# Order of the start of a fused FFT and gated-FFN kernel: weight pieces, E sums and copies of batch 0 laid out anew

## The chip, the cores and the metric

The kernel runs on one core of one Trainium2 chip. The metric is the device time of one execution in microseconds (us). Before the change three runs gave 1927.33, 1927.47 and 1928.5 us, with a median of 1927.47 us. One further execution was profiled; every duration below is from it.

## The reference

```python
X = np.fft.fft(x, axis=1)          # x: 8 batches, 3008 positions, 256 features
X = np.fft.fft(X, axis=2).real
y = X.reshape(24064, 256)
gate = 1 / (1 + np.exp(-(y @ w_gate)))      # 256 x 1536
val = y @ w_val                             # 256 x 1536
out = (gate * val) @ w_out                  # 1536 x 256
```

The weights arrive as 64-bit floats and are turned into 32-bit floats on the chip.

## The kernel before, in words

**The algebra.** The transform over the features (`dt`, 256 x 256) is multiplied into the weights first: a "piece" `merge` (L346) is four matmuls of `dt` with one 256 x 256 block of a weight, into one PSUM bank `ps`, and `merged` (L353) copies the bank into the SBUF tile `G`. The transform over the positions is done by folding `x` (sums and differences of mirrored rows) and multiplying it with tables `st` of cosines and sines; the results are `pk` and `qk`. A tile of the gate then needs G times pk (`front_a`, L729) and G times qk (`front_b`, L740), both added in one bank `pf`.

**The weights.** There are 18 jobs: 0 to 11 are the pieces of gate and value in turn, 12 to 17 are blocks of `w_out`. A job goes through `weight_load` (L257, a transfer of 512 KB on the SP queue), `weight_parts` (L303, two ScalarE instructions L309 and L311), `weight_join` (L313, three VectorE instructions L322, L323, L325 and one GpSimd add L327), and for jobs 0 to 11 the piece. `ge_load` (L371) then sends two rows of `G` by two small transfers per job into the columns `ge`.

**Batch 0.** Its `x` comes in three thirds, each with its part of the two tables. For each third, `folds[2*j]` is `third` (L496: L498, L499 and two L460, all VectorE) and `folds[2*j+1]` is `feats` and `turned` (L503 on VectorE; L510 and L513 are ScalarE copies with a sign into the tile `XV`, which lies in the table's space `st`, and into `x`). Then TensorE adds the third's sums into the six banks of three `seq_group`s (rows `ev` and `od`). A fourth group (second block of qk) is summed after the last third. Each group is then read out by one ScalarE copy (L576) and two VectorE operations (L582, L586).

**The E row.** One feature column, number 128, is summed apart: `e0_sums` (L605) is eight matmuls per third with one output row each, into the bank `pe`; `e0_heads` (L634) is three VectorE copies and two sums for the first 252 positions (`eh`), `e0_spread` (L646) spreads them over 128 partitions by one matmul (row `ek`) and one copy; `e0_copies` (L619) reads out the whole row by four ScalarE copies, and `e0_row` (L626) puts it together on GpSimd, from where it goes to memory `ed` and comes back for the later position groups (`e_rows`, L711).

**The loop.** From L1114 on, `i` counts tiles of 128 of the 1536 inner features. In each turn stand `front_a(i)`, `gate_a(i-1)` (L745: a sigmoid L752 and a difference `z` L753), `part(i)` (L734: a copy `ae` of the bank, L738), `seed(i+1)` (L720: two ScalarE instructions L727 that start the bank with ek times ge), `gate_b(i-1)` (L760: L765, L766, L769), then what three tables `mid`, `use` and `pre` put at this turn (joins, pieces, parts of later jobs), the output matmuls, and `front_b(i)`.

**Order.** The kernel sets the order by hand: each of the five engines runs its instructions in the order in which the code issues them, and waits for semaphores. The transfers go through the SP queue; each takes one of eight completion slots in turn, and so is issued only when the eighth before it has landed. PSUM has eight banks: `po0` to `po4` are named, three more (`x`) go round.

Of the kernel before, what the change touches and what calls it, by code (L numbers as in the profile page):

```python
# [82 lines left out]
def kernel(  # L83
# [10 lines left out]
    nc = tc.nc  # L94
# [345 lines left out]
    def fold_ops(b, nq):  # L440
# [25 lines left out]
        if b:  # L466

            for i in (0, 2):
                e = nc.vector if b == 1 else pool
                ops += [lambda i=i, q=q, e=e: point(e, i, i + 1, q) for q in qs]  # L470
                ops.append(lambda i=i, e=e: first(e, i, i + 1, slice(0, NQ)))
            for blk in range(2):
                ops += [lambda blk=blk, q=q: across(pool, blk, q) for q in qs]
            ops += [lambda q=q: feat(pool, *parts[1], q) for q in qs]
            for i, op in enumerate((ALU.add, ALU.subtract)):
                for ds in (slice(0, HD), slice(HD, D)):
                    ops.append(lambda i=i, op=op, ds=ds: pool.tensor_tensor(
                        x4[:, 3, i * N3 : (i + 1) * N3, ds], x4[:, 1, 0:N3, ds],
                        x4[:, 1, N3:, ds], op=op))
            parts[0] = x4[:, 3], x4[:, 1]  # L480
            slots = x4.rearrange("p i q d -> p (i q) d")

            def turn(q, minus):

                y = [slots[:, q : q + 16 : 15], slots[:, q + N3 : q + N3 + 10 : 9]]
                if minus:
                    y.reverse()
                nc.vector.scalar_tensor_tensor(
                    out=y[0][:, :, HD:D], in0=y[1][:, :, 0:HD], scalar=(ST[3], ST[4])[minus][:, q : q + 1],
                    in1=y[0][:, :, 0:HD], op0=ALU.mult, op1=ALU.add)  # L490
            TURN[b] = [lambda q=q, minus=minus: turn(q, minus) for q in range(N3) for minus in range(2)]
            ops += [lambda q=q: feat(pool, *parts[0], q) for q in qs]
        else:
            tt = nc.vector.tensor_tensor

            def third(q):  # L496
                a, m = x4[:, 0:3:2, q], x4[:, 1:4:2, q]
                tt(a[:, :, :, 0], a[:, :, :, 0], m[:, :, :, 0], op=ALU.add)  # L498
                tt(a[:, :, :, 1:D], a[:, :, :, 1:D], m[:, :, :, D - 1 : 0 : -1], op=ALU.add)  # L499
                across(nc.vector, 0, q)  # L500
                across(nc.vector, 1, q)

            def feats(q):  # L503
                v, r = x4[:, 0:2, q], x4[:, 2:4, q]
                nc.vector.memset(r[:, :, :, 0:1], 0.0)
                lo, hi = v[:, :, :, 1:HD], v[:, :, :, D - 1 : HD : -1]
                tt(r[:, :, :, 1:HD], lo, hi, op=ALU.subtract)
                tt(lo, lo, hi, op=ALU.add)
            def turned(q):
                copy = lambda to, of, s: nc.scalar.activation(to, of, AF.Copy, scale=s)  # L510
                copy(XV[:, :, q], x4[:, 1::-1, q, 0 : HD + 1], sign(q.start))
                for i in range(q.start, q.stop):
                    copy(x4[:, 3:1:-1, i, HD:D], x4[:, 3:1:-1, i, 0:HD], sign(i, True))  # L513
            XR_[0] = [(XV[:, i], x4[:, 3 - i, :, HD:D]) for i in range(2)]
            for q in qs:
                ops += [lambda q=q: third(q), lambda q=q: (feats(q), turned(q))]
        for blk, (v, r) in enumerate(parts):
            if b and blk:
                W[b, blk] = v[:, :, HD:D], r[:, :, HD:D]
# [85 lines left out]
    def e0_sums(j):  # L605

        if not j:
            E0["ps"] = bank("pe", 3)
        for q in (2 * j, 2 * j + 1):
            for blk in range(2):  # L610
                row = (2 * blk + q % 2) * TB
                mm(E0["ps"][row : row + 1, columns(blk)[0]], W[0, blk][2][:, q], table_of(0, q, blk), not j, j == N3 - 1)
        for q in (2 * j, 2 * j + 1):
            for blk in range(2):
                row = (2 * blk + q % 2) * TB
                mm(E0["ps"][row : row + 1, columns(blk)[1]], XV[:, blk, q, HD : HD + 1],
                   table_of(0, q, blk, True), False, j == N3 - 1)
# [326 lines left out]
    nc.gpsimd.dma_start(out=zero, in_=nil)  # L944
    nc.scalar.dma_start(out=dt, in_=dtab.rearrange("(c p) d -> p c d", p=P))
    load_x(0)
    for j in range(3):
        weight_load(j)
    for j in range(N3):
        load_third(j)  # L950
        for t in range(2):
            load_table(t, j)
        weight_load(3) if not j else None
    for j in (4, 5):
        weight_load(j)

# [6 lines left out]
    def piece(j, other=None):  # L963
        merge(WS.pop(j), *jobs[j], other)

    shared["er"] = pqp.tile([P, NK + 1], F32, name="er", tag="pk")[0:1]
    signs()
    warm(12)
    for j in range(3):
        weight_parts(j)  # L970
        weight_join(j, NB - 1)
        piece(j)
    for j in range(2):
        merged(j)
        ge_load(j)
    seq_start(0)
    folds = fold_ops(0, 2)
# [1 line left out]
    halves.append(seq_group(0, 0, 1))  # L979
    for j in range(N3):  # L980
        folds[2 * j]()
        if not j:
            weight_parts(3)
            merged(2)
        folds[2 * j + 1]()
        for sums, _, _ in halves:
            sums(2 * j, 2 * j + 1)
        if not j:
            weight_join(3, NB - 1)
            piece(3)  # L990
            merged(3)
            for i in (6, 7):
                weight_load(i)
            ge_load(2)
            ge_load(3)
            for i in (8, 9, 12, 10, 11):
                weight_load(i)
    weight_parts(4)
    halves[0][1]()()
    weight_join(4, NB - 1)  # L1000
    weight_parts(5)
    halves[1][1]()()
    weight_join(5, NB - 1)
    halves[2][1]()()
    halves = [seq_group(0, 1, 1, (0, 1))]
    halves[0][0](*range(NQ))
    for j in range(N3):
        e0_sums(j)
    weight_parts(6)
    weight_join(6, NB - 1)  # L1010
    e0_heads()
    weight_parts(7)
    weight_join(7, NB - 1)
    halves[0][1]()()
    e0_copies()
    piece(4)
    e0_spread(2)
    piece(5)
    merged(4)
    weight_parts(8)  # L1020
    weight_join(8, NB - 1)
    piece(6)
    seed(0)
    merged(5)
    seed(1)
    front_a(0)
    for i in (14, 15):
        weight_load(i)
    merged(6)
    seed(2)  # L1030
    part(0)
    piece(7, 1)
    front_a(1)
    part(1)
    weight_parts(9)
    front_a(2)
    merged(7)
    for i in (13, 16, 17):
# [8 lines left out]
        side.setdefault(i, []).extend(fs)  # L1047


    at(0, e0_row, lambda: nc.sync.dma_start(out=ed[0:1], in_=shared["er"]))  # L1050
    pre, use, mid = {}, {}, {}
    def using(j):
        weight_use(j, j % 2)
        if jobs[j][0] < 2:
            merged(j)
    for j, i in ((9, 0), (10, 1), (11, 2), (12, 3), (13, 5), (14, 6), (15, 8), (16, 10), (17, 12)):
        if j > 9:
            pre.setdefault(i - 1, []).append(lambda j=j: weight_parts(j))
        mid.setdefault(i, []).append(lambda j=j: weight_join(j, 2))
        if jobs[j][0] == 2:  # L1060
            use.setdefault(i + 2, []).append(lambda j=j: using(j))
# [17 lines left out]
    at(3 * i0 + 6, table_again)  # L1079
    at(4 * i0 + 5, lambda: [at(4 * i0 + i, f) for i, f in zip((6, 7, 8, 9, 10, 7), table_odd())])  # L1080
    for i in range(i0, count, i0):
        at(i - 11, lambda i=i: e_rows(i))

    for b in range(B - 1):
        s0 = b * per
# [114 lines left out]
```

## Time and profile before

| | |
|---|---|
| profiled execution, time | 1927.12 us |
| its span, first to last instruction | 1925.3 us |
| median of three other runs | 1927.47 us |
| granted TensorE clock, mean | 0.999 |
| TensorE busy | 1912.3 us, 99% |
| first 60 us: TensorE busy | 51.91 us |
| first 60 us: transfers, GB/s by tens of us | 293, 330, 341, 296, 259, 1 |

A timeline row gives the start in us from the span's start, the time taken, the engine, the line, the operation, output <- inputs, and how many records follow each other; in square brackets stands the idle time of that engine before the row and who ended it. One 32-bit matmul is two records on TensorE. All TensorE instructions have line L135, so they are known by their output: `ps` pieces, `ev` and `od` sums, `pe` and `ek` the E row, `pf<-pk` front_a, `pf<-qk` front_b.

### The profile page before, as it was taken

How to read it: one execution, taken by the hardware profiler on the slowest of the kernel's cores; microseconds unless marked ns; L12 is line 12 of the kernel's file. 1: busy time of each engine (PE TensorE's matmuls, PEld its weight loads, DVE VectorE, ACT ScalarE, POOL GpSimd, SP SyncE). 2: the span in 40 equal slices, each digit the busy share in tenths (PEclk: the TensorE clock that was granted, in tenths of full speed). 3: DMA queues.
4: the chain of work that ended last, by engine and by line, in shares of the span. 5: the costliest groups of instructions: out<-in, count | busy, mean ns of one | idle time of the engine just before them, and what ended most of it. 6: DMA issues, size and time to landing. Idle time of an engine off the chain costs nothing.

```text
span 1925.3 us, 34658 instructions
## 1 busy us (share of the span) xinstructions
PE 1912.3 (99%) x11340; PEld 1793.2 (93%) x11340; DVE 1413.4 (73%) x3220; ACT 1346.8 (70%) x3155; POOL 1556.9 (81%) x2807
## 2 busy tenths in 40 slices
PE   8999999999999999999999999999999999999999
PEld 7899999999999999999999999999999999999998
DVE  7757877787767776777777777777777777766776
ACT  5877767767777677776777767777677766777775
POOL 2489989978898688986888868888788886777775
PEclk9999999999999999999999999999999999999999
DMA  9251421111021201202111021111200100000001
GB/s 315 66 98 37 107 80 55 53 50 44 20 75 27 80 17 30 75 14 80 24 47 51 20 81 22 47 49 25 80 15 15 25 17 15 15 22 20 26 17 30
DMA packets 169215, 95.62 MB, mean 50 GB/s; under 512 B 129658, under 2 KB 159940, under 8 KB 167244
## 3 DMA queue, kind: packets, MB, share of 16 engines
q1 hardware_dynamic: 168482, 92.90, 17.0%
q8 instruction: 91, 1.49, 0.3%
q14 instruction: 88, 0.72, 0.1%
q10 hardware_dynamic: 522, 0.50, 0.1%
q0 software_dynamic: 32, 0.00, 0.0%
HBM read 68.13 MB, written 47.24 MB: 60 GB/s over the span
## 4 chain that ended last, share of the span: by engine, by line
PE 97%; DVE 1%; POOL 1%; ACT 1%; DMA 0%; issue 0%; ACTq 0%; DVEq 0%; POOLq 0%
PE pf L135 50%; PE po L135 41%; PE ev L135 3%; PE rows L135 1%; PE od L135 1%; PE row L135 0%; PE ps L135 0%; DVE x L460 0%; POOL sf L775 0%; PE pe L135 0%; DMA raw<-in_moe_w_gate_dram 0%; DVE join L323 0%; DVE join L322 0%; DVE x L499 0%; DVE raw L325 0%
## 5 line engine op out<-in xcount | busy, mean ns | idle before, releaser
L775 POOL TENSOR_TENSOR sf<-h 128x168 f32<-128x168 f32 (+1 forms) x935 | 517.6, 573 | 228.8 <-DVE h L769 228.2
L775 POOL TENSOR_TENSOR sf<-h,sf 128x168 f32<-128x168 f32 (+1 forms) x1122 | 615.3, 570 | 49.0 <-DVE h L769 47.6
L135 PE MATMUL pf<-pk,G 128*128 128x252 f32 (+1 forms) x2304 | 582.8, 376 | 0.5 <-ACT pf L727 0.4
L135 PE MATMUL pf<-qk,G 128*128 128x252 f32 (+1 forms) x2304 | 582.0, 375 | 0.1
L727 ACT ACTIVATE pf<-ek,ge 128x252 f32<-128x252 f32 (+1 forms) x1152 | 542.7, 471 | 19.3 <-DVE h L769 0.3
L769 DVE TENSOR_TENSOR h<-pf,z 128x252 f32<-128x252 f32 (+1 forms) x576 | 241.5, 419 | 412.6 <-ACT pf L766 410.9
L135 PE MATMUL po<-sf,wf 128*128 128x168 f32 (+1 forms) x2992 | 517.0, 306 | 0.3 <-POOL sf L775 0.2
L738 ACT ACTIVATE ae<-pf 128x504 f32<-128x504 f32 (+1 forms) x576 | 339.8, 590 | 247.7 <-PE pf L135 246.0
L135 PEld LDWEIGHTS pf<-pk,G 128*128 128x128 f32 x2304 | 436.9, 190 | 52.9 <-issue 2.0
L135 PEld LDWEIGHTS po<-sf,wf 128*128 128x128 f32 x2992 | 460.5, 190 | 9.2 <-POOL sf L775 1.2
L135 PE MATMUL po<-h,wf 128*128 128x168 f32 (+1 forms) x2618 | 463.4, 305 | 0.0
L135 PEld LDWEIGHTS pf<-qk,G 128*128 128x128 f32 x2304 | 410.9, 190 | 26.3 <-ACT ae L738 0.5
L135 PEld LDWEIGHTS po<-h,wf 128*128 128x128 f32 x2618 | 416.6, 190 | 16.2
L753 DVE TENSOR_TENSOR z<-ae,pf 128x504 f32<-128x504 f32 (+1 forms) x576 | 386.0, 670 | 61.9 <-ACT h L752 57.3
L893 DVE TENSOR_TENSOR c<-c 128x168 f32<-128x168 f32 (+1 forms) x929 | 425.1, 466 | 3.4
L752 ACT ACTIVATE h<-pf 128x252 f32<-128x252 f32 (+1 forms) x576 | 219.0, 380 | 208.4 <-PE pf L135 199.5
L765 DVE TENSOR_TENSOR h<-h,pf 128x252 f32<-128x252 f32 (+1 forms) x576 | 233.3, 405 | 0.0
L766 ACT ACTIVATE pf<-z 128x252 f32<-128x252 f32 (+1 forms) x576 | 211.6, 367 | 23.0 <-DVE h L765 19.2
L775 POOL TENSOR_TENSOR sf<-sf 128x168 f32<-128x168 f32 (+1 forms) x187 | 104.4, 558 | 14.7
L775 POOL TENSOR_TENSOR sf<-sf,h 128x168 f32<-128x168 f32 (+1 forms) x187 | 110.5, 591 | 0.0
L806 ACT COPY c<-po 128x504 f32<-128x504 f32 (+1 forms) x141 | 80.0, 568 | 0.0
L902 DVE STREAM_TRANSPOSE os<-c 128x256 f32<-128x256 f32 x184 | 79.9, 434 | 0.0
(167 smaller groups left out, 923.9 us busy)
## 6 DMA issues: line engine op xcount, KB each, us to landing
x<-xr SPq DMA_DIRECT2D x14, 1536.0 KB
out_dram<-os SPq DMA_DIRECT2D x368, 56.0 KB
xr<-in_xf_dram SPq DMA_DIRECT2D x14, 768.0 KB
xr<-in_xf_dram SPq DMA_DIRECT2D x35, 256.0 KB
ek<-ed SPq DMA_DIRECT2D x39, 126.0 KB
out_dram<-os SPq DMA_DIRECT2D x284, 7.0 KB
x<-in_xf_dram SPq DMA_DIRECT2D x3, 1024.0 KB
st<-in_stab_dram SPq DMA_DIRECT2D x4, 564.8 KB
```

The source lines that it names most:

```text
L135: nc.tensor.matmul(o, l, r, start=start, stop=stop, skip_group_check=True)
L727: nc.scalar.activation(PF[i][:, g], EK[i // NFT], AF.Copy, scale=ge[:, g, f : f + 1])
L738: nc.scalar.activation(AP[i], PF[i], AF.Copy, scale=2.0)
L752: nc.scalar.activation(H[p][:, fh, 0:n], PF[i][:, 0], AF.Sigmoid)
L753: nc.vector.tensor_tensor(z[:, :, ::-1], AP.pop(i), PF[i], op=ALU.subtract)
L765: nc.vector.tensor_tensor(h[:, fh, 0:n], h[:, fh, 0:n], pf[:, 1], op=ALU.mult)
L766: nc.scalar.activation(pf[:, 0], z[:, 0], AF.Sigmoid)
L769: nc.vector.tensor_tensor(h[:, fh, n:], pf[:, 0], z[:, 1], op=ALU.mult)
L775: nc.gpsimd.tensor_tensor(block(p, dst), block(p, a), block(p, b), op=(ALU.subtract, ALU.add)[op])
L806: (nc.vector.tensor_copy if t == 1 or t == 3 and not last else nc.scalar.copy)(C[0][:, 3 * t * R : 3 * (t + 1) * R], PO[t][:, 0 : 3 * R])
L893: engine.tensor_tensor(t[:, dst * R : (dst + 1) * R], *v, op=(ALU.subtract, ALU.add)[op])
L902: nc.vector.transpose(os_[0][:, s, 0:nb, h, :], t[:, c0 : c0 + nb * TB])
```

## The change

It moves instructions among the engines' queues in the first 70 us, and splits one copy in two. No matmul, no VectorE instruction and no byte of transfer is added or left out; ScalarE gets three instructions more.

1. Jobs 0 to 3 are loaded, joined and multiplied ahead of the first third of `x`. Before, job 3 was loaded behind third one and its tables, and its parts, join and piece stood between thirds one and two.
2. `e0_sums(j)` stands inside third j, between `third` and `feats`; before, all three came after the fourth group. For this, `turned` leaves out column 128 and a new ScalarE instruction copies it right after `third`. `e0_heads` follows the last third; `e0_copies` comes some steps earlier.
3. The eight ge transfers of jobs 0 to 3 are issued ahead of the loads of jobs 6 to 12; before, four of them came behind jobs 6 and 7. Job 12 is loaded behind 10 and 11.
4. The parts of job 4 stand ahead of the last third's copies, the joins of jobs 4 and 5 have a bank of the round, and pieces 4, 5 and 6 follow each other.
5. Parts and joins of jobs 9 and 10 stand ahead of the first gate; before, job 9's join was in turn 0 and job 10's in turn 1. Job 11's goes from turn 2 to turn 1.
6. `e0_row` and its transfer move from turn 0 to turn 4, the first `e_rows` from turn 1 to turn 5.

```diff
-                copy(XV[:, :, q], x4[:, 1::-1, q, 0 : HD + 1], sign(q.start))
+                copy(XV[:, :, q, 0:HD], x4[:, 1::-1, q, 0:HD], sign(q.start))
...
-                ops += [lambda q=q: third(q), lambda q=q: (feats(q), turned(q))]
+                ops += [lambda q=q: (third(q), nc.scalar.activation(
+                            XV[:, :, q, HD], x4[:, 1::-1, q, HD], AF.Copy, scale=sign(q.start))),
+                        lambda q=q: (feats(q), turned(q))]
...
-            E0["ps"] = bank("pe", 3)
+            E0["ps"] = bank("pe", NB - 1)
...
-    for j in range(3):
+    for j in range(4):
         weight_load(j)
...
-        weight_load(3) if not j else None
...
+    for j in range(4):
+        weight_parts(j)
+        weight_join(j, j % 3)
+        piece(j, (None, None, None, 3)[j])
+        if j > 1:
+            merged(j - 2)
+    merged(2)
     for j in range(3):
-        weight_parts(j)
-        weight_join(j, NB - 1)
-        piece(j)
-    for j in range(2):
-        merged(j)
         ge_load(j)
...
         folds[2 * j]()
+        e0_sums(j)
         if not j:
-            weight_parts(3)
-            merged(2)
+            merged(3)
+            ge_load(3)
+            for i in (6, 7, 8, 9, 10, 11, 12):
+                weight_load(i)
         folds[2 * j + 1]()
+        if j == 1:
+            weight_parts(4)
         for sums, _, _ in halves:
             sums(2 * j, 2 * j + 1)
-        if not j:
-            weight_join(3, NB - 1)
-            piece(3)
-            merged(3)
-            for i in (6, 7):
-                weight_load(i)
-            ge_load(2)
-            ge_load(3)
-            for i in (8, 9, 12, 10, 11):
-                weight_load(i)
-    weight_parts(4)
+    e0_heads()
+    weight_join(4)
     halves[0][1]()()
-    weight_join(4, NB - 1)
     weight_parts(5)
+    weight_join(5)
     halves[1][1]()()
-    weight_join(5, NB - 1)
     halves[2][1]()()
     halves = [seq_group(0, 1, 1, (0, 1))]
     halves[0][0](*range(NQ))
-    for j in range(N3):
-        e0_sums(j)
     weight_parts(6)
+    e0_copies()
     weight_join(6, NB - 1)
-    e0_heads()
     weight_parts(7)
     weight_join(7, NB - 1)
     halves[0][1]()()
-    e0_copies()
-    piece(4)
     e0_spread(2)
-    piece(5)
-    merged(4)
     weight_parts(8)
     weight_join(8, NB - 1)
-    piece(6)
+    for j in (4, 5, 6):
+        piece(j)
+    merged(4)
     seed(0)
+    weight_parts(9)
+    weight_join(9, NB - 1)
     merged(5)
     seed(1)
     front_a(0)
+    merged(6)
+    seed(2)
+    piece(7, 1)
+    front_a(1)
+    weight_parts(10)
+    weight_join(10, NB - 1)
+    part(0)
+    part(1)
     for i in (14, 15):
         weight_load(i)
-    merged(6)
-    seed(2)
-    part(0)
-    piece(7, 1)
-    front_a(1)
-    part(1)
-    weight_parts(9)
     front_a(2)
...
-    at(0, e0_row, lambda: nc.sync.dma_start(out=ed[0:1], in_=shared["er"]))
+    at(4, e0_row, lambda: nc.sync.dma_start(out=ed[0:1], in_=shared["er"]))
...
-    for j, i in ((9, 0), (10, 1), (11, 2), (12, 3), (13, 5), (14, 6), (15, 8), (16, 10), (17, 12)):
-        if j > 9:
+    for j, i in ((11, 1), (12, 3), (13, 5), (14, 6), (15, 8), (16, 10), (17, 12)):
+        if j > 10:
...
-        at(i - 11, lambda i=i: e_rows(i))
+        at(i - (11 if i > i0 else 7), lambda i=i: e_rows(i))
```

## The prediction

> **What bounds the kernel now.** First the page's busy line, then the windows of the whole span, then the timeline of TensorE and that of VectorE over the first 90 us.
>
> ```profile
> PE 1912.3 (99%) x11340; PEld 1793.2 (93%) x11340; DVE 1413.4 (73%) x3220; ACT 1346.8 (70%) x3155; POOL 1556.9 (81%) x2807
> ```
>
> TensorE is busy all the time but 13 us. The windows (busy us and records of PE, PEld, DVE, ACT, POOL; clock; DMA share; GB/s) say where those are:
>
> ```profile
> 10.00:20.00 10.00, 7.83 (x38) 6.12 (x37) 9.71 (x17) 4.39 (x8) 4.11 (x3) 1.00 1.07 330
> 40.00:50.00 10.00, 8.11 (x37) 6.28 (x36) 6.93 (x14) 7.98 (x17) 3.86 (x3) 1.00 0.73 259
> 50.00:60.00 10.00, 8.76 (x39) 6.82 (x38) 7.37 (x13) 8.32 (x19) 5.92 (x7) 1.00 0.03 1
> 80.00:90.00 10.00, 10.00 (x48) 8.84 (x47) 7.57 (x15) 8.65 (x22) 6.07 (x9) 1.00 0.11 39
> ```
>
> Before 60 us TensorE has gaps, after it none until the tail. TensorE's timeline shows where the gapless part begins:
>
> ```profile
> 28.32 0.58 PE L135 MATMUL ev<-st,x 126*128 126x189 f32 x2
> 38.45 1.99 PE L135 MATMUL ps<-wqk,dt 128*128 128x256 f32 x8
> 42.19 0.66 PE L135 MATMUL ek<-eh,busy 1*128 1x252 f32 x2 [1.75 <-DVE eh L644]
> 46.64 1.12 PE L135 MATMUL pf<-pk,G 128*128 128x252 f32 x4
> ...
> 61.87 1.12 PE L135 MATMUL pf<-qk,G 128*128 128x252 f32 x4
> 65.42 1.01 PE L135 MATMUL pf<-qk,G 128*128 128x252 f32 x4
> 68.85 1.01 PE L135 MATMUL pf<-qk,G 128*128 128x252 f32 x4
> 72.27 1.01 PE L135 MATMUL pf<-qk,G 128*128 128x252 f32 x4
> ```
>
> The row at 61.87 is the fourth front_b; from it on a turn takes 3.43 us, which is its matmuls alone (0.85 + 0.85 + 1.73). So **my yardstick is the start of the fourth front_b**: if it comes a microsecond earlier, the end does too. What sets it is on VectorE:
>
> ```profile
> 20.32 2.39 DVE L460 TENSOR_TENSOR x<-x 126x512 f32<-126x512 f32 x2
> 25.40 1.42 DVE L460 TENSOR_TENSOR x<-x 126x512 f32<-126x512 f32 x2
> 27.57 0.69 DVE L508 TENSOR_TENSOR x<-x 126x508 f32<-126x508 f32 x1
> 31.46 0.55 DVE L582 TENSOR_TENSOR pk<-a,od 128x377 f32<-128x377 f32 x1 [3.20 <-ACT a L576]
> ...
> 51.55 0.69 DVE L322 TENSOR_SCALAR join<-wc 128x512 f32<-128x512 f32 x1 [4.21 <-ACT wc L309]
> ...
> 54.00 0.68 DVE L753 TENSOR_TENSOR z<-ae,pf 128x504 f32<-128x504 f32 x1 [0.30 <-ACT h L752]
> ```
>
> From 5.28 to 28.26 VectorE never pauses; from there to the first gate (`z` at 54.00, L753) it idles 3.20 + 0.17 + 4.21 + 0.30 = 7.9 us. From `z` to the yardstick are 7.87 us.
>
> **The change, part by part.** Times are places in the span.
>
> *Job 3 ahead of third one.* Its load (about 1.1 us of transfer) goes in front of third one, which landed at 10.53 by the trace's completion times and now lands near 11.7; the sum of bytes ahead of third two is as before. ScalarE's parts of job 3 wait behind the first `merged` (10.95 to 11.54), end at 12.1, and the join runs 12.15 to 14.2 (2.06, as at 16.94 to 19.00). Third one then takes its 5.15 us (11.87 to 17.02) and ends at 19.4 instead of 17.02: **2.4 us later**. Third two needs no join ahead of it and starts at 19.35 instead of 19.00.
>
> In thirds one and two the two L460 take 2.37 and 2.39 us, in third three 1.42; only in the first two does job 2's or 3's GpSimd add L327 run beside them, and it takes 2.23 us instead of 1.29. After the change only third one has an add beside it, so third two takes 4.2 us (as third three) and ends at 23.6. [...]
>
> *E sums inside the thirds.* Now TensorE is the chain: sums of third one 19.45, 4.06 long (17.07 to 21.13); E sums of third two, 2.03 / 3 = 0.68; sums of third two 4.11 (24.21 to 28.32); E sums of third three 0.68; sums of third three 4.19; fourth group 3.91. The split adds a wait: the instruction list has the copies L510 wait for TensorE's reads of the split-off column, some 0.3 us in thirds two and three. That is 19.45 + 4.06 + 0.68 + 4.41 + 0.68 = 29.3 for the last E sum and 37.7 for the fourth group, whereas before the fourth group and the E sums ended at 38.45. The E sums' price is bounded by nothing below (hidden by `feats`) and by eight ordinary sums (8 x 0.32 = 2.6 us a third) above; I take 0.68, their own row. Each new copy of one column costs ScalarE 0.2 to 0.5 (its 2x1 activation and its 126x256 copies); third one's is hidden, third three's stands behind job 4's parts, whose transfer landed at 27.17 (parts to 28.35, copy to 28.6): just in time.
>
> *VectorE to the first gate.* E heads come at once, at 29.3. Then, with spacings of the rows: heads 1.46, joins 4 to 10 with 2.05 each before a group's results and 2.2 before another join (14.9 in all), eight results L582 and L586 (0.93 a pair, 3.7). That is 20.1 us, so 49.4 without a pause. ScalarE is as full: its copy of the E row waits for the second group's results (36.7), and behind it stand parts 7, 8, 9, 10, 11 (1.16 each), two small copies (0.64), three times `merged` and `seed` (1.53), two `ae` (0.98), a `merged` (0.48) and the first sigmoid (0.4) besides its own 0.48: 13.4 us, to 50.1. **So the first `z` is at 50.1 instead of 54.00.** In other words, some 6 us of VectorE's idle go, and job 10's join, 2.1 us, comes in front.
>
> *From `z` on.* `z` 0.72, `ae` 0.50, sigmoid 0.40, L769 0.33, job 11's join 2.07, next `z` 0.59, L765 0.45, sigmoid 0.27, `merged` 0.50, parts of job 12 1.16, sigmoid 0.29, `ae` 0.63: 7.9, as before. The fourth front_b starts at 58.0. TensorE alone would be there earlier: 37.7, then E spread 0.43, seven pieces 12.1, four front_a 3.4 and three front_b 2.55, in all 56.2. So the gates' chain is late next, TensorE pausing about 1.8 us.
>
> *At no cost.* Eight ge transfers now stand on SP ahead of job 6: the last waits for the slot of job 5 (28.70), so job 6 is issued near 29.3 instead of 25.02 and, as job 8 did (30.53 to 34.75), lands at 33.5 instead of 30.15; its parts are due at 34.8 and its join at 37.6, and job 7's later. That is 1.3 us of cover. Jobs 8 to 12 land between 36 and 42, each over 2 us before its parts. `e0_row` (four GpSimd operations, 3.5 us, 55.11 to 58.5) made job 10's add late by 0.35 us; in turn 4 it stands between adds due two turns (6.9 us) later, and the row read back is due in turn 11, 20 us on. The joins' other banks are free by then.
>
> **Sum:** 61.87 - 58.0 = 3.9, less 0.1 because the walk by these rows is no finer: 3.8 us. From the profiled 1927.12 that is 1923.3; the median of the runs is 0.35 higher, so 1923.6.
>
> **Rivals.**
> *More.* If ScalarE's order costs less than the rows say, TensorE's 56.2 is the end of it: 5.7 us, 1921.8. Against it: ScalarE has no slack from 36.7 to 50.1. Chance 0.15.
> *Job 6 late.* If its landing is past 34.8 plus the join's slack, each us goes to the end; at 2 to 3 us more of delay, 1925 to 1926. For it: SP issues in order and ge transfers took up to 1.4 us each; against: 1.3 us to spare on ScalarE, 2 on VectorE. Chance 0.13.
> *The E sums cost more on TensorE* (twice their row: 0.7 more for each of two): 1925.0. Chance 0.10.
> *Slower.* Job 4's parts stand on ScalarE ahead of the copies that the last third's sums need, and wait for its transfer. Before it landed at 27.17 and was not used until 29.86. Beyond 28 each microsecond of it delays everything, and past 31.8 the kernel is slower: at 33 it is 1928.8. That needs transfers at 290 GB/s where the windows show 330 and 341. [...] Chance 0.05.
> *No effect.* A wait behind 62 us takes the gain back: 1927.1 to 1927.5. Against it: TensorE has no pause from 62 to 180 us, so nothing there is late by less than the 3.8 us. Chance 0.02.
>
> **How the numbers follow.** Forecast, 3.2 to 4.4 us of gain (1923.0 to 1924.2), 0.55; the others as given. 0.2% of 1927.47 is 3.86 us, about what a measurement here can tell from no change, and the forecast lies on that edge: half of it, 0.28, and "more" are faster by over 0.2%, 0.43; the other half, with the two smaller gains and no effect, is within, 0.52; slower 0.05. The range takes in the rivals but the slow one and the far end of "more": 1922.2 to 1926.0.
>
> **What would show it.** Right: the E heads at about 29.3 on VectorE, no idle of over 1 us from there to the first `z` at about 50, the fourth front_b at about 58, then turns of 3.43. Wrong: ScalarE's L309 waiting for a transfer between 28 and 45, sums of third three beginning after 30, or a pause on TensorE after 62.

## The result and the profile after

The changed kernel takes 1924.82 us (median of 22 runs, 1924.26 to 1925.69), the kernel before on the same chip 1927.47 us (22 runs, 1927.08 to 1928.83). The medians differ by 2.65 us, where 3.8 were forecast; the ratio of the runs is 0.9985, 95% interval 0.9978 to 0.9992. The profiled execution took 1925.47 us, 1.65 us less than that of before; it is one of the longer ones of the changed kernel. Two single runs, one of an experiment and one of the kernel before beside another, took 2216 and 2217 us at a granted clock of 0.85, and are left out.

Two functions have grown by two lines, so lines behind L510 are two higher: the new copies of the split-off column are L516, the group results L578, L584 and L588, `z` is L755 and `ae` L740. Of the page, TensorE's total is what it was:

```profile
PE 1912.1 (99%) x11340; PEld 1793.4 (93%) x11340; DVE 1410.9 (73%) x3220; ACT 1346.3 (70%) x3158; POOL 1554.7 (81%) x2807
```

So the change can only have closed pauses of TensorE. The windows of the changed kernel (busy us and records of PE, PEld, DVE, ACT, POOL; clock; DMA share; GB/s) say where:

```profile
10.00:20.00 10.00, 8.20 (x48) 5.60 (x47) 9.12 (x17) 3.82 (x8) 4.80 (x3) 1.00 1.06 315
20.00:30.00 10.00, 9.68 (x72) 7.83 (x72) 7.79 (x13) 3.65 (x8) 0.00 (x0) 1.00 0.93 277
30.00:40.00 10.00, 8.81 (x57) 7.98 (x58) 8.04 (x18) 8.13 (x18) 2.60 (x2) 1.00 0.72 256
40.00:50.00 10.00, 10.00 (x46) 8.30 (x45) 9.40 (x16) 9.78 (x21) 4.21 (x4) 1.00 1.02 377
50.00:60.00 10.00, 8.89 (x41) 7.52 (x40) 6.78 (x13) 7.43 (x17) 3.54 (x3) 1.00 0.04 1
```

Between 40 and 50 us TensorE is now full (8.11 before) and VectorE works 9.40 us (6.93 before). Between 30 and 40 it is not: 8.81. TensorE's timeline of the changed kernel shows the hole, and the yardstick:

```profile
17.11 1.99 PE L135 MATMUL ps<-wqk,dt 128*128 128x256 f32 x8 [1.68 <-POOL wqk L327]
...
19.84 0.59 PE L135 MATMUL ev<-st,x 126*128 126x189 f32 x2
...
29.26 0.50 PE L135 MATMUL pe<-st,x 126*1 126x189 f32 x8
31.12 0.50 PE L135 MATMUL pe<-st 126*1 126x188 f32 x8 [1.36 <-ACT st L516]
...
60.20 1.12 PE L135 MATMUL pf<-qk,G 128*128 128x252 f32 x4 [1.32 <-ACT ae L740]
...
63.76 1.01 PE L135 MATMUL pf<-qk,G 128*128 128x252 f32 x4
...
67.18 1.01 PE L135 MATMUL pf<-qk,G 128*128 128x252 f32 x4
```

The fourth front_b starts at 60.20 instead of 61.87, 1.67 us earlier, and the time is 1.65 us less: the yardstick held. It holds in all fourteen profiles of this case: from that start to the end of the span they take 1863.37 to 1863.52 us. But 58.0 was forecast. The loss is at 31.12, where the last third's second half of E sums waits for the column copy L516. ScalarE's timeline tells why it was late:

```profile
29.68 0.66 ACT L309 ACTIVATE wqk<-raw 128x512 f32<-128x512 f32 x1 [3.06 <-DMA raw<-in_moe_w_gate_dram]
30.24 0.64 ACT L311 ACTIVATE raw<-raw 128x512 int32<-128x512 uint32 x1
30.78 0.29 ACT L516 ACTIVATE st<-x,sgn 126x4 f32<-126x4 f32 x1
```

L309 and L311 are job 4's parts. They stand ahead of L516 and wait until job 4's transfer is down: 29.66 by the trace's completion times, against 27.17 before. In the kernel before they stood behind the last third's copies, and waited for nothing. ScalarE's timeline of before:

```profile
29.86 0.65 ACT L309 ACTIVATE wqk<-raw 128x512 f32<-128x512 f32 x1
```

VectorE of the changed kernel shows the rest of the chain:

```profile
15.96 2.38 DVE L460 TENSOR_TENSOR x<-x 126x512 f32<-126x512 f32 x2
...
21.02 1.42 DVE L460 TENSOR_TENSOR x<-x 126x512 f32<-126x512 f32 x2
...
25.11 0.17 DVE L498 TENSOR_TENSOR x<-x 126x4 f32<-126x4 f32 x1 [1.23 <-DMA x<-in_xf_dram]
...
31.74 0.59 DVE L644 COPY er<-pe 1x126 f32<-1x126 f32 x2 [2.43 <-PE pe L135]
...
52.37 0.68 DVE L755 TENSOR_TENSOR z<-ae,pf 128x504 f32<-128x504 f32 x1 [0.52 <-ACT h L754]
```

The same row of the kernel before:

```profile
40.52 0.59 DVE L642 COPY er<-pe 1x126 f32<-1x126 f32 x2
```

The E heads start at 31.74 (before 40.52, forecast 29.3), and 20.63 us later stands the first `z` (forecast 20.8). The wait of 1.23 us for third three's `x` is new but off the path: the sums of the second third hold TensorE until 29.2 anyway.

### The profile page after: what moved, and what is told of

Read it like the earlier page. It is cut to its first block, busy times and chain, and to the rows that moved or that the text cites. A ratio compares the mean times of both kernels' runs of the same rounds, so it can differ in the third digit from the quotient of the medians.

```text
span 1923.7 us, 34664 instructions
## 1 busy us (share of the span) xinstructions
PE 1912.1 (99%) x11340; PEld 1793.4 (93%) x11340; DVE 1410.9 (73%) x3220; ACT 1346.3 (70%) x3158; POOL 1554.7 (81%) x2807
## 3 DMA queue, kind: packets, MB, share of 16 engines
q8 instruction: 91, 1.49, 0.3%
## 4 chain that ended last, share of the span: by engine, by line
PE 96%; ACT 1%; POOL 0%; DVE 0%; issue 0%; ACTq 0%; POOLq 0%
PE pf L135 50%; PE po L135 41%; PE ev L135 2%; PE rows L135 1%; PE od L135 1%; PE row L135 0%; POOL sf L777 0%; ACT pf L729 0%; ACT G L358 0%; ACT ae L740 0%; PE pe L135 0%; ACT wf L311 0%; ACT wc L311 0%; PE ps L135 0%; POOL st L231 0%
## 5 line engine op out<-in xcount | busy, mean ns | idle before, releaser
L740 ACT ACTIVATE ae<-pf 128x504 f32<-128x504 f32 (+1 forms) x576 | 339.2, 589 | 249.2 <-PE pf L135 248.0
L135 PEld LDWEIGHTS pf<-qk,G 128*128 128x128 f32 x2304 | 410.8, 190 | 27.9 <-ACT ae L740 2.1
L755 DVE TENSOR_TENSOR z<-ae,pf 128x504 f32<-128x504 f32 (+1 forms) x576 | 386.0, 670 | 63.1 <-ACT h L754 58.3
```

The source lines that it names most:

```text
L135: nc.tensor.matmul(o, l, r, start=start, stop=stop, skip_group_check=True)
L740: nc.scalar.activation(AP[i], PF[i], AF.Copy, scale=2.0)
L755: nc.vector.tensor_tensor(z[:, :, ::-1], AP.pop(i), PF[i], op=ALU.subtract)
```

## The experiments

All are edits of the changed kernel unless another is named. Each was timed in 11 runs and profiled once, in three groups on three chips. The kernel before was timed with each group; its shortest times there are 1926.95, 1927.00 and 1927.15 us, against 1927.08 beside the result. So a difference of medians of less than some 0.3 us says nothing here.

One number helps to read the profiles. In the changed kernel the E heads stand 28.46 us ahead of the fourth front_b. In the eight experiments below that leave the order behind the heads as it is, and in which VectorE finds the parts of job 4 ready, it is 28.48 to 28.60. So in these the start of the E heads alone sets the time.

### 1 to 4: the wait for job 4

Three theories stood against each other at first. A: the loss is job 4's parts on ScalarE, which wait for their transfer with the last third's copies behind them. B: the transfers as a whole are late, the last third of `x` too, wherever the parts stand. C: the gates' chain behind the E heads is full and takes as long wherever it starts.

**load4_early**, job 4's load ahead of the last third of `x`:

```diff
     for j in range(N3):
         load_third(j)
...
-    for j in (4, 5):
-        weight_load(j)
+        weight_load(4) if j == 1 else None
+    weight_load(5)
```

> The changed kernel, with job 4's load issued ahead of the last third of x instead of behind it; nothing else differs. Theory A (the missing microsecond is ScalarE: job 4's parts wait for their transfer, with the last third's copies behind them): the wait of 1.36 us on TensorE between the two halves of the last E sums is gone, the first z comes near 51, and the time falls by about 1.0 us against the changed kernel, to some 3.5 us below the kernel before. Theory B (transfers were slow as a whole in that execution, and the last third of x, which VectorE awaited for 1.23 us, is what counts): x is 1.2 us later still, and the time rises by about 1 us. Theory C (the gates' chain is full whenever it starts): no difference.

Measured: 1924.90 us (1924.43 to 1926.91). ScalarE no longer waits for a transfer, but in the profiled execution (1925.50) the E heads still started at 31.77. There the time went earlier, into job 3's piece. TensorE's timeline of load4_early, and the window of the same stretch:

```profile
17.05 3.42 PE L135 MATMUL ps<-wqk,dt 128*128 128x256 f32 x8 [2.02 <-POOL wqk L327]
```
```profile
17.00:20.40 3.40, 3.35 (x8) 2.21 (x9) 3.29 (x7) 0.30 (x1) 0.00 (x0) 0.57 1.08 290
```

The same eight matmuls take 3.42 us instead of 1.99, 0.43 each instead of 0.22, and the granted clock of the window is 0.57 (0.52 from 18 to 21 us): behind a pause of 2.02 us it was at about half for most of the piece. So this profile says nothing on A against B. The median fits neither: A asked for 1 us less, B for 1 us more. It opened a theory G, that the clock costs something in some executions.

**load4_late**, job 4's load behind job 5's:

```diff
-    for j in (4, 5):
+    for j in (5, 4):
```

> The changed kernel, with the loads of jobs 4 and 5 in the other order, so that job 4 lands some 1.2 us later and everything else as before. Theory A (job 4's parts on ScalarE hold the last third's copies): TensorE's wait inside the last E sums grows from 1.36 to about 2.6 us and the time rises by 0.9 to 1.3 us against the changed kernel, to about 1.5 us below the kernel before. Theory B (the last third of x counts): no difference. Theory C (the gates' chain is full whenever it starts): no difference.

Measured: 1926.88 us (1925.53 to 1928.22), so 2.1 us slower in the median, more than A's 0.9 to 1.3. The wait grows, as A alone says, but to 2.07 us instead of 2.6; the profiled execution, 1926.00, is only 0.5 longer than that of the changed kernel. TensorE's timeline of load4_late:

```profile
31.70 0.50 PE L135 MATMUL pe<-st 126*1 126x188 f32 x8 [2.07 <-ACT st L516]
```

**parts4_behind**, the parts behind the last third's copies, the load as in the changed kernel:

```diff
-        if j == 1:
+        if j == 2:
             weight_parts(4)
```

> The changed kernel, with ScalarE's parts of job 4 behind the last third's copies instead of ahead of them. Theory A: TensorE's wait inside the last E sums is gone and the E heads come 1.5 us earlier, but job 4's join now waits for parts that come after the copies (near 31 us), so that most of it is given back: between 0.2 us faster and 1.4 us slower than the changed kernel. Theory B (the last third of x counts): no difference. Theory C (the gates' chain is full whenever it starts): no difference.

Measured: 1924.49 us (1924.34 to 1924.84, and one run of 1926.38). No E sum waits any more. VectorE's timeline of parts4_behind:

```profile
29.82 0.59 DVE L644 COPY er<-pe 1x126 f32<-1x126 f32 x2 [1.95 <-PE pe L135]
...
31.93 0.69 DVE L322 TENSOR_SCALAR join<-wqk 128x512 f32<-128x512 f32 x1 [0.71 <-ACT wqk L309]
...
51.28 0.68 DVE L755 TENSOR_TENSOR z<-ae,pf 128x504 f32<-128x504 f32 x1 [0.54 <-ACT h L754]
```

The heads come 1.9 us earlier than in the changed kernel, the join of job 4 gives 0.71 back since its parts are now late, and the profiled execution is 1.1 us shorter (1924.37). The median gains only 0.3, but ten of eleven times lie within 0.5 us, where the changed kernel's 22 spread over 1.4: what the wait cost seems to vary from execution to execution, and the best times of the two kernels are the same (1924.26 and 1924.34). With load4_late this supports A against B and C, both of which asked for no difference. Part of C holds: from the heads on, the chain takes as long wherever it starts.

**jobs_9_10_back**, jobs 9 and 10 where they were:

```diff
-    weight_parts(9)
-    weight_join(9, NB - 1)
...
-    weight_parts(10)
-    weight_join(10, NB - 1)
...
-    for j, i in ((11, 1), (12, 3), (13, 5), (14, 6), (15, 8), (16, 10), (17, 12)):
-        if j > 10:
+    for j, i in ((9, 0), (10, 1), (11, 2), (12, 3), (13, 5), (14, 6), (15, 8), (16, 10), (17, 12)):
+        if j > 9:
```

> The changed kernel, with parts and joins of jobs 9, 10 and 11 back in the turns 0, 1 and 2, as in the kernel before. If putting them ahead of the gates was worth what the prediction says (VectorE's idle of 4.2 us filled, 2.1 us of join paid ahead): near 0.6 us slower than the changed kernel, with VectorE idle ahead of job 9's join. Rival: ScalarE is full up to the first gate either way and the order does not matter: no difference. Other rival: the joins would be better off among the gates, where TensorE hides them: faster by 1 us or more.

Measured: 1925.20 us (1924.30 to 1926.08), 0.4 slower in the median, which the spreads don't separate from nothing. In its profile VectorE idles 3.14 us ahead of 49.23 for the parts that were put back. The fourth front_b is at 59.55, since the E heads come at 30.53; but from the heads to it are 29.01 us instead of 28.46. So the two joins ahead of the gates are worth 0.55 us in the profiles, as the expectation said.

### 5 to 7: which part brings the gain, and why the transfer is late

**esums_behind**, the E sums and heads back behind the fourth group:

```diff
         folds[2 * j]()
-        e0_sums(j)
...
-    e0_heads()
...
     halves[0][0](*range(NQ))
+    for j in range(N3):
+        e0_sums(j)
+    e0_heads()
```

> The changed kernel with the three e0_sums and e0_heads put back behind the fourth group; all else as changed. Theory A (the E sums inside the thirds are what brings the gain, since VectorE then has work where it idled): E heads near 38 instead of 31.7, VectorE idle again, first z near 55, fourth front_b near 63, and as job 10's join now stands in front of it, 4 to 5 us slower than the changed kernel: 1929 to 1930. Rival D (the gain comes from the pieces ahead of the thirds and from the parts' order): 1925 to 1926. On job 4's transfer, theory F (it lands late because TensorE's next instructions are fetched by the same DMA engines at 23 to 25 us, earlier than in the kernel before, as the E sums use them up sooner): without the E sums the fetch is at 27 to 29 again, the transfer lands near 27.2 in all its sixteen parts, and the copies of the last third do not wait for it. Rival B (the loads as a whole are late by the new order of the loads): it lands at 28.4 or later here too, and L309 waits for a DMA.

Measured: 1928.43 us (1927.79 to 1928.76), 3.6 slower than the changed kernel, where A asked for 4 to 5, and no faster than the kernel before (1928.39 on the same chip). VectorE's and TensorE's timelines of esums_behind:

```profile
39.38 0.59 DVE L644 COPY er<-pe 1x126 f32<-1x126 f32 x2 [3.35 <-PE pe L135]
...
55.36 0.68 DVE L755 TENSOR_TENSOR z<-ae,pf 128x504 f32<-128x504 f32 x1 [0.77 <-ACT h L754]
```
```profile
40.95 0.66 PE L135 MATMUL ek<-eh,busy 1*128 1x252 f32 x2 [1.64 <-DVE eh L646]
41.54 2.86 PE L135 MATMUL ps<-wqk,dt 128*128 128x256 f32 x8
```

VectorE idles 3.35 us again, and TensorE pauses before `ek`; the eight matmuls of the piece behind that pause take 2.86 us instead of 1.99, the clock being 0.64 from 41.5 to 45 us (0.59 from 42 to 45). So some 0.9 of the difference in this profile is the clock's. Without the E sums inside the thirds all the rest of the change brings nothing; rival D falls.

On the transfer: in the kernel before, job 4 landed at 27.17, and at 28.34 started the first of the packets that the profile counts as queue q8, kind "instruction": 16 KB, 1.0 us there, 1.4 in the changed kernel. It is called the fetch here, as it is taken for a fetch of TensorE's next instructions. That is inferred: the run has 91 such packets, one for some 250 of TensorE's 22,680 records.

- In the three profiles without E sums inside the thirds (before, esums_behind, before_warm) the fetch comes at 28.34 to 28.84. In the eleven with them it comes at 23.33 to 26.92. So the change brings it forward; something else moves it too, by 1.8 us (23.35 to 25.18) with the same instructions.
- In five profiles with the fetch between 24.9 and 25.9 (parts4_behind, jobs_9_10_back, warm_wide, pause_warm, job3_back) the parts of job 4's transfer that move together were down at 27.1 to 27.6, and one alone was 1.3 to 1.5 us later, at 28.4 to 29.1.
- In esums_behind and before_warm none came alone, and all were down by 27.75. That lies between theory F's 27.2 and rival B's 28.4, nearer to F; L309 still waited 2.54 us for the transfer in esums_behind.
- With the fetch at 23.3 to 23.5 (the changed kernel, column_apart, between_warm) all parts were late, 27.9 to 29.7; only in the changed kernel was the last one alone, by 0.8 us.

So one part of the delay is probably the fetch; the trace doesn't tell which DMA engine carried which packet, so this rests on the times alone and is an inference. The DMA strips from 22 to 27 us, in 40 slices, of before and then of the changed kernel, show the other part:

```profile
GB/s 377 361 410 311 377 299 361 331 351 338 338 338 326 326 326 350 338 338 326 338 338 314 338 322 415 330 380 295 393 344 360 360 328 410 311 393 311 393 360 360
```
```profile
GB/s 442 344 459 344 459 360 442 377 377 393 424 356 339 363 334 197 258 217 205 253 314 242 254 265 241 253 278 265 229 241 338 283 296 277 367 249 237 270 258 311
...
q8 instruction: 1, 0.02, 1.7%
```

In the changed kernel the rate falls from some 390 to some 260 GB/s half a microsecond behind the fetch (q8 is its queue) and stays low. That is not the fetch's doing alone: in column_wide (below) the rate was as low, 268 GB/s from 24 to 27 us, with the fetch only at 26.92, and the parts were down at 28.9, the last one at 30.15. Why the transfers run slower in some executions is not settled.

**warm_wide**, the warm matmuls in half as many instructions, to move the fetch:

```diff
-            mm(ps[:, 0:CH], busy[:, 0:P], busy, True, True)
+            mm(ps[:, 0 : 2 * CH].rearrange("p (i c) -> p i c", i=2), busy[:, 0:P],
+               busy.unsqueeze(1).to_broadcast([P, 2, CH]), True, True)
...
-    warm(12)
+    warm(6)
```

> The changed kernel with its twelve first matmuls of 252 columns (which only warm TensorE) written as six of 504: the same columns, but 12 matmul records and 12 weight loads fewer ahead of the fetch. Theory F: the fetch starts some 2 us later (25 to 27 instead of 23.35); if that is near the transfer's end, the wait of L516 and the matmul behind it shrinks from 1.36 us to under 0.5 and the time by 0.3 to 1 us: 1923.8 to 1924.5. Rival B: the transfer lands at 28.4 to 29.7 all the same and nothing changes: 1924.8.

Measured: 1924.45 us (ten runs of 1923.52 to 1925.31), 0.4 less. The fetch came at 25.42, and TensorE's wait was 0.70 instead of 1.36, where F asked for under 0.5. TensorE's timeline of warm_wide:

```profile
30.15 0.50 PE L135 MATMUL pe<-st 126*1 126x188 f32 x8 [0.70 <-ACT st L516]
```

That agrees with the fetch's share, weakly: kernels without this edit had their fetch at 24.9 to 25.2 too.

### 8 to 10: the split copy, and two rivals that fell

**column_apart**, the split-off column in a tile of its own, so that L510 need not wait for TensorE's reads of it:

```diff
+    XC = const.tile([P, 2, NQ], F32, name="xc")
...
-                            XV[:, :, q, HD], x4[:, 1::-1, q, HD], AF.Copy, scale=sign(q.start))),
+                            XC[0:NP, :, q], x4[:, 1::-1, q, HD], AF.Copy, scale=sign(q.start))),
...
-                mm(E0["ps"][row : row + 1, columns(blk)[1]], XV[:, blk, q, HD : HD + 1],
+                mm(E0["ps"][row : row + 1, columns(blk)[1]], XC[0:NP, blk, q : q + 1],
```

> The changed kernel with the split-off E column in a tile of its own, so that the copies L510 no longer wait for TensorE's reads of it. If the split's wait costs what the prediction said (0.3 us in each of thirds two and three), 0.2 to 0.5 us faster than the changed kernel wherever job 4's transfer does not set the third: 1924.4 (0.0 to 0.5 less). If job 4's parts set the last third anyway: no change, 1924.8.

Measured: 1925.92 us (1924.28 to 1927.58): 1.1 slower, against the expectation. What was meant to happen did happen: from E sums to E sums the thirds take 4.94 and 4.78 us instead of 5.11. But the tile's 48 bytes in a partition move the addresses of the tiles behind it, and the packets of 2 KB take 87.3 ns (mean from 5 to 11 us), against 84.0 to 84.9 in the thirteen other profiles; the rate from 5 to 10 us is 391 GB/s, against 407 in the changed kernel. What made the runs slower no trace shows: the profiled execution, 1924.28, is the shortest of the eleven, and it has the slower packets.

**column_wide**, the same with 256 bytes (in both, line numbers are one higher still):

```diff
-    XC = const.tile([P, 2, NQ], F32, name="xc")
+    XC = const.tile([P, 2, 32], F32, name="xc")
```

> As column_apart, but the column's tile is 256 bytes wide in a partition instead of 48. Theory K: column_apart was slower (1925.9) only because its 48 bytes move all tiles behind it off a multiple of 64 bytes, which slows the transfers' packets (87 to 88 ns instead of 84 from 6 to 11 us of its profile); then here packets take 84 ns again and the time is 0.0 to 0.5 us under the changed kernel's: 1924.4. Rival: the tile of its own costs by itself (the copy or its reads): 1925.5 to 1926.5 again, with packets of 84 ns.

Measured: 1924.41 us (1923.14 to 1925.99), packets at 84.2 ns. So the slower packets and the 1.5 us between the two medians both went with the address; that the one made the other is not shown. The profiled execution was the slowest of the eleven, and shows a clock of about half once more (0.58, and 0.51 from 18 to 21 us). TensorE's timeline of column_wide and its window:

```profile
17.08 3.36 PE L135 MATMUL ps<-wqk,dt 128*128 128x256 f32 x8 [1.88 <-POOL wqk L328]
```
```profile
17.00:20.40 3.40, 3.32 (x12) 2.20 (x16) 3.29 (x7) 0.30 (x1) 0.03 (x1) 0.58 1.04 294
```

**job3_back**, job 3 between thirds one and two again:

```diff
-    for j in range(4):
+    for j in range(3):
         weight_load(j)
...
+        weight_load(3) if not j else None
...
-    for j in range(4):
+    for j in range(3):
...
-        piece(j, (None, None, None, 3)[j])
+        piece(j)
...
-    merged(2)
-    for j in range(3):
+    merged(1)
+    for j in range(2):
...
         if not j:
-            merged(3)
-            ge_load(3)
-            for i in (6, 7, 8, 9, 10, 11, 12):
-                weight_load(i)
+            weight_parts(3)
+            merged(2)
...
+        if not j:
+            weight_join(3)
+            piece(3)
+            merged(3)
+            ge_load(2)
+            ge_load(3)
+            for i in (6, 7, 8, 9, 10, 11, 12):
+                weight_load(i)
```

> The changed kernel with job 3 (load, parts, join, piece, merged) and ge 2 back between thirds one and two; E sums, parts of job 4 and pieces 9 and 10 as changed. By the prediction's steps: third one's sums 2.4 us earlier (near 17.1 to 17.4), but third two has the join (2.06) and a GpSimd add beside its L460 (2.38 instead of 1.42) again, and TensorE has piece 3 (1.99) between the sums, so that the E heads come 0 to 0.6 us later than without a wait for job 4 (29.8): 1924.8 to 1925.4. Rival D (job 3 ahead of the thirds is what brings the gain, the E sums little): E heads past 33, and 1926.5 or more. Rival H (job 3 ahead costs more than it brings, by the pause that it opens on TensorE ahead of piece 3): faster than the changed kernel, 1924 or less.

Measured: 1924.69 us (ten runs of 1924.24 to 1925.58, and one of 1928.47), no difference to the changed kernel. The sums of third one start at 16.92, 2.9 us earlier, the E heads at 31.21. Rival D asked for 1926.5 or more, H for 1924 or less; both fall: the fourth piece ahead of the thirds neither brings nor costs anything that shows.

### 11 and 12: the clock, and a better version

**pause_warm**, four warm matmuls in the pause ahead of piece 3:

```diff
+        warm(4) if j == 3 else None
         piece(j, (None, None, None, 3)[j])
```

> The changed kernel with four more warm matmuls (8 records, some 1.7 us) in TensorE's pause ahead of piece 3. Theory G (in some executions the granted clock is halved behind that pause, as in the profile of load4_early, where it was 0.57 from 17 to 20.4 us behind 2.02 us of pause, and job 3's eight matmuls took 0.43 us each instead of 0.22): the times above 1925.3 go, spread under 0.7 us, median 1924.5. Rival: the clock is not what spreads the times; the median and spread stay (1924.8, 1.4 us), or rise by up to 0.3 as the fetch comes some 1.3 us earlier.

Measured: 1924.90 us (ten runs of 1923.85 to 1925.50, one of 1927.15). The pause is filled and the clock 1.00, but the spread stays: theory G does not explain it. The wait for job 4 fits it better: in parts4_behind and in between_warm (below), where no E sum waits, nearly all times lie within 0.5 us.

**before_warm**, the same filler in the kernel before, ahead of `ek`:

```diff
     piece(4)
+    warm(4, 2)
     e0_spread(2)
```

> The kernel before with four warm matmuls (8 records, 1.7 us) in TensorE's pause of 1.75 us ahead of ek, and nothing else. Its times fall in two groups, 1927.0 to 1927.4 and 1928.3 to 1928.8. Theory G: the upper group are executions in which the granted clock is halved behind this pause (as in the profile of esums_behind, 0.59 from 42 to 45 us behind a pause of 1.64); then the upper group goes, and nearly all times lie at 1927.0 to 1927.4. Rival: the two groups have another cause (transfers): both stay, in about the shares of the kernel before on the same chip.

Measured: 1927.59 us (1927.18 to 1928.61). Six of eleven runs lie under 1927.8, against ten of 33 of the kernel before on that chip. The upper group is still there; with these numbers it can't be said whether the filler thinned it.

**between_warm**, job 4's parts between the last column copy and the last third's other copies, with the filler ahead of piece 3:

```diff
+        warm(4) if j == 3 else None
         piece(j, (None, None, None, 3)[j])
...
         e0_sums(j)
+        if j == 2:
+            weight_parts(4)
...
-        if j == 1:
-            weight_parts(4)
```

> The changed kernel with two edits: job 4's parts stand on ScalarE between the last third's column copy L516 and its copies L510 (where ScalarE waited 1.76 us for TensorE in the run with the parts behind), so that the column copy and the E sums no longer wait for job 4's transfer; and four warm matmuls in TensorE's pause ahead of piece 3. Theory A: E sums without a wait, E heads near 29.8, no wait of join 4 if the transfer is down by 28.6, first z near 50.6, fourth front_b near 58.4: 1923.6 to 1924.2, and the times lie closer together (within 0.8 us) than the changed kernel's 1.4. If the transfer is down at 29.7, L510 is late by 1 us, but the sums that need its copies come 0.75 us after the first ones: 1924.5. Rival: the last third's wait only moves to the sums behind L510, no gain: 1924.8.

Measured: 1924.04 us (1923.80 to 1924.32), ratio to the kernel before 0.9978 (0.9969 to 0.9987, with 1928.50 us for the kernel before on that chip): the shortest median and the narrowest spread, 0.5 us, of all. Of its two edits the filler alone (pause_warm) moved nothing, so the gain goes to the place of the parts. ScalarE's timeline of between_warm:

```profile
28.34 0.30 ACT L516 ACTIVATE st<-x,sgn 126x4 f32<-126x4 f32 x1 [1.52 <-PE od L135]
29.27 0.69 ACT L309 ACTIVATE wqk<-raw 128x512 f32<-128x512 f32 x1 [0.62 <-DMA raw<-in_moe_w_gate_dram]
29.86 0.65 ACT L311 ACTIVATE raw<-raw 128x512 int32<-128x512 uint32 x1
30.41 0.72 ACT L510 ACTIVATE st<-x,sgn 126x512 f32<-126x512 f32 x1
```

Job 4's transfer was late here too (29.25), but L516 no longer stands behind it, and the parts fill the time in which ScalarE waited 1.76 us for TensorE. The E heads start at 30.41 and the fourth front_b at 59.00. The expectation named 29.8 and 58.4; the time is inside its 1923.6 to 1924.2. Four other profiles (parts4_behind, column_apart, warm_wide, pause_warm) have 59.0 to 59.3 as well.

## Why the prediction was right, and where it fell short

The time is inside the range and the mechanism is the one forecast; the size is off by 1.2 us in the medians and 2.2 in the profiles. The range was met by luck in part: 1924.82 lies outside the forecast's own 1923.0 to 1924.2, in a stretch that the range took in for two rivals (job 6 late, dear E sums) that did not occur. By its steps, in the profiled execution:

- **The yardstick** held: 1.67 us at the fourth front_b, 1.65 in the time, turns of 3.43 behind it.
- **Job 3 ahead of third one** was sized right. Third one ended at 19.78 instead of 19.4, because the first transfer of job 0 was down at 4.97 instead of 4.55 in this execution (4.50 to 4.69 in esums_behind, column_apart, warm_wide and pause_warm, whose sums of third one start at 19.53 to 19.69): 0.39 of the 2.2 us. The L460 took 2.38, 1.42 and 1.42 us: only third one, which has a GpSimd add beside it (L327, 2.23 us from 14.83), was slow, as the thirds with an add were before (2.37 and 2.39 against 1.42). In job3_back, where job 3's add runs beside third two again (GpSimd busy 2.21 us from 18 to 24 us), its L460 took 2.38.
- **The E sums' price** was right within 0.25 us: 9.42 us from the sums of third one to the last E sums instead of 9.17. The split's wait of some 0.3 us shows in column_apart, where the thirds are 0.17 and 0.33 shorter without it. The rival of dear E sums did not occur; its 1925.0 is near the measured time by chance.
- **Job 4's parts, "just in time"**, is the step that failed. It took the transfer's landing of before, 27.17, as given; it landed at 29.66, and the last E sum took 1.80 us longer than its 0.68: 1.36 of wait, the rest the end of the second half behind it. The place of the wait and its mechanism are those of the rival "slower", at a smaller price: the rival's 31.8 was not reached. Its chance of 0.05 was far too low for a landing beyond 28: in all nine profiles with the E sums inside the thirds and job 4 loaded where the change has it, the transfer was down at 28.41 to 30.15. What moved the landing is probably in part the change itself, which brings the packet taken for an instruction fetch forward into the transfer (23.35 instead of 28.34); the rest is open. (The rival's 1928.8 for a landing at 33 should read some 1928.6 by its own step, 1923.6 + 5.)
- **E heads to first `z`** was right: 20.63 instead of 20.8, VectorE with no idle over 0.52 us. **`z` to the yardstick** too: 7.83 instead of 7.9. TensorE paused 1.32 us for `ae`, where 1.8 was forecast, so the gates' chain is what sets the end, as forecast.
- **At no cost** held. Job 6 was issued at 31.50 instead of 29.3 and was down at 35.88; its parts started at 36.60 without a wait, 0.7 us of cover instead of 1.3. The rival "job 6 late" did not occur.

The terms add up: 0.39 + 0.25 + 1.80 - 0.17 - 0.07 = 2.20, the distance from 58.0 to 60.20. With the wait gone (parts4_behind, between_warm), the fourth front_b is at 59.1 and 59.0, so about half of the 2.2 us is recovered. What is left to 58.0 is, in the one, the E heads at 29.82 instead of 29.3 and the 0.7 us before join 4, and in the other the late start of third one (sums at 19.99 instead of 19.45) and the rest of the heads' 30.41.

The forecast has no term for the clock, which was 1.00 across the pauses of before in its first 60 us, the longest of them 1.75. The later runs show a lower one: 0.57, 0.58 and 0.64 as means over windows of 3.4 to 3.5 us behind pauses of 2.02, 1.88 and 1.64 us (load4_early, column_wide, esums_behind), at a price of 1.43, 1.37 and 0.87 us for the piece behind them. Behind 2.07 (load4_late, ahead of 31.70), 1.84, 1.78, 1.75, 1.69 and four times 1.68 us it stayed at 1.00, so length alone does not decide.

How long it lasted is an estimate from windows of 3 us. In load4_early they have 0.91 from 15 to 18 us and 0.52 from 18 to 21, in column_wide 0.92 and 0.51, in esums_behind 0.59 from 42 to 45 and 0.85 from 45 to 48, and 1.00 on either side. If the clock was either 1.00 or about half (the eight matmuls took 0.43 us each instead of 0.22), it was at half for some 3.4 us in each of the three, beginning 0.4, 0.4 and 1.6 us after the pause's end. Why it fell there and not behind the pauses of 1.84 and 1.78 us, which are longer than the 1.64, is open.

## What to carry to other kernels

A transfer's landing time in one trace is no constant to build on: before an instruction that waits for it is put ahead of copies on the critical path, give it the spread that several profiles show (here 28.41 to 30.15 in nine profiles of kernels that load job 4 alike, and 27.17 in the trace that the forecast used), not one trace's value. The wait is cheap to disarm: put the dependent work into a gap in which its engine waits anyway, behind what others need first. A gain of one part (here the E sums inside the thirds, 3.6 us) is found by undoing each part alone. The other parts of a large edit may be worth little: here two joins ahead of the gates 0.55 us in the profiles, and the fourth piece ahead of the thirds nothing. Where medians are too coarse for that, the distance between two rows of the profile, one ahead of the part and one behind it, still shows it.

## What the hardware showed that was not expected

- The profile's queue q8, kind "instruction", has 91 packets of 16 KB, 1.49 MB in the whole run, each 0.9 to 1.5 us, before and after the change; that they are TensorE's rests on their count alone. In five profiles a transfer under way then had one of its sixteen parts 1.3 to 1.5 us late, and its completion with it; that the packet made it late is inferred from the times.
- The granted clock was 0.57 to 0.64, as means over 3.4 to 3.5 us, behind pauses of 1.64 to 2.02 us in three of the fourteen profiled executions, and the change opens such a pause (1.68 us, with the clock at 1.00 behind it in this profile) ahead of piece 3 where before the longest up to 30 us was 1.21.
- With tiles moved by 48 bytes in a partition, packets of 2 KB were 4% slower (87.3 instead of 84.0 ns, one profile); with 256 bytes they were not (84.2).
